# Attention ahead of two gated MLPs: normalization steps at the end of a turn, and weight decodes inside the turns

## The chip, the core and the metric

The kernel runs on one core of one Trainium2 chip. The metric is the device time of one execution in microseconds (us); lower is better. The engines are named as the profile names them: PE (TensorE matmul) and PEld (its weight loads), DVE (VectorE), ACT (ScalarE), POOL (GpSimd) and SP (SyncE, which issues nearly all DMAs here).

## The reference

Attention over 4 batches of 12 heads, 448 positions, head size 64; then two gated MLPs on 1792 tokens with 768 columns inside and 1536 hidden ones.

```python
def rmsnorm(x, g):
    rms = np.sqrt(np.mean(x * x, axis=-1, keepdims=True) + 1e-06)
    return x / rms * g
q_n, k_n = rmsnorm(q, g_q), rmsnorm(k, g_k)
scores = scale * np.matmul(q_n, k_n.transpose(0, 1, 3, 2))
scores = scores - np.max(scores, axis=-1, keepdims=True)
attn = np.exp(scores)
attn = attn / (np.sum(attn, axis=-1, keepdims=True) + 1e-09)
attn_out = np.matmul(attn, v)
...
x = (x @ w_a) * (x @ w_b) @ w_out                                # first MLP
x = (1 / (1 + np.exp(-(x @ w_gate)))) * (x @ w_val) @ w_out      # second MLP
```

The weights arrive as 64-bit floats, which the kernel reads as pairs of 32-bit words.

## The kernel before

**Attention in turns.** Two heads of one batch form a pair; there are 24 pairs. A table of steps, `turns`, is played once for each i from 1 to 22; `begin` stands before it and `end` behind it. A step is a small function with an offset: `(exp, 0, 4)` works on pair i, `(x_tr, -1, 0, 0)` on pair i-1. No scheduler moves anything: the order of the table is the order of the instructions on every engine, and each engine works strictly in order.

The steps of a pair, in the order of its life:

- `load`, `load_r`, `load_v` (SP): q, k and v.
- `squares` (POOL, L192 to L196): products and a first halving of the sum. L192 is one multiplication of 768 columns.
- `mean` (DVE, L203 reduces, L204 scales and adds), `rsqrt` (ACT, L211 Ln, L212 Exp), `newton` (DVE, L219 to L221): together the factor `y` of the normalization.
- `scale` (POOL, L230 and L243): q and k times `y`, into `qkn` and `qrem`. `t_tr` (PE, L254 to L259) transposes them into a PSUM buffer of the ring `tr`, which has 3 buffers.
- `k_hi` and `q_hi` (ACT, L278 and L264) and `k_lo` and `q_lo` (DVE, L288 and L269) split them into a high and a low part KH, KL, QH, QL. `k_ends` (POOL, L294) copies two small corners of KH and of KL.
- `s` (PE, L305): scores of one or two row tiles; `top` (DVE, L311): the negated row maximum `nm`; `exp` (ACT, L323): the exponentials P and their sums. The scores `s` have 4 PSUM banks for 7 tiles a turn, so a bank must be free of its `exp` before it is written again.
- A turn later, `x_tr` (PE, L333 to L341) transposes P into the ring `tr`; `x_out` copies it to SBUF, on ACT (L352) or on DVE (L350). `pv` (PE, L365) multiplies with v.
- `rsum` (DVE, L372 adds 1e-9 to 7 sums a row, L373 takes the reciprocal), `rsum_tr` (PE, L379), `rsum_post` (ACT, L384, then a DMA of the row to DRAM), `rsum_get` (SP, L393, three DMAs that broadcast it), `norm` (DVE, L400: `xs` = `pv` times `rs`) and `put` (SP, L405).
- `early_hi` and `early_lo` (ACT L422, POOL L428) prepare a first part of the MLP's input in six of the turns.

**Weights.** A quarter of a weight block (128x384) is loaded as `raw` (L611, 384 KB) and decoded: one ACT operation (L622), then L623, L625 and L629 on DVE. A decoded quarter, or a difference of two, is then split into `wh` (ACT, L717) and `wl` (DVE, L559). `prepare(l, e, n)` advances two generators, `decodes` and `splits`, by n small pieces; a whole decode takes four pieces. It decodes up to the eighth quarter and splits up to the fourth product before the MLP has begun. `decode` (L434) is the step that calls it; before, it stands ten times in `end`, and nowhere else. A `raw` is loaded when a decode ends, and waits on SP for the buffer that this decode read.

**MLP.** `first_part` walks over products (m, p), each 18 matmuls (L870) of a block of weights with one of seven combinations of the input's quadrants (a Strassen scheme). The first eight products need only inputs that attention has long stored; the ninth needs S1, the sum of two quadrants (`operands`, DVE L783, with the casts of L774 and the rests of L559). The quadrants come back from DRAM (`stage_in`, L755), some of them behind the last pair's `norm` and `put`.

Of the kernel before, what the change touches and what calls it, by code (L numbers as in the profile page):

```python
# [23 lines left out]
def attention_then_two_gated_mlps(  # L24
# [90 lines left out]
    def attention():  # L115
# [316 lines left out]
            begin_u()  # L432

        def decode(i, n):  # L434
            prepare(0, 3, 1)

        def close_s(i):
            sctx.close()
# [6 lines left out]
        def mlp(i, n):  # L445
# [11 lines left out]
            (exp, 0, 1), (top, 0, 5), (scale, 2, 1), (k_lo, 1), (k_ends, 1), (exp, 0, 5), (s, 0, 2), (s, 0, 3), (load, 4),  # L457
            (scale, 2, 0), (scale, 2, 2), (top, 0, 2), (load_r, 3), (exp, 0, 2), (top, 0, 6), (squares, 3),
            (exp, 0, 6), (top, 0, 3), (t_tr, 2, 1), (t_tr, 2, 0), (exp, 0, 3), (mean, 3), (k_hi, 2), (k_lo, 2),
            (q_hi, 2), (q_lo, 2), (k_ends, 2),  # L460
        )

        turns = (
            (rsum_get, -2), (early, 0), (put, -3), (s, 0, 0), (rsqrt, 2), (s, 0, 1), (newton, 2),
            (x_tr, -1, 0, 0), (x_tr, -1, 0, 1), (top, 0, 0), (exp, 0, 0), (rsum, -1), (x_out, -1, 0, 0), (top, 0, 4),
            (exp, 0, 4), (x_out, -1, 0, 1), (pv, -2, 1), (scale, 2, 1), (scale, 2, 0), (scale, 2, 2), (top, 0, 1),
            (exp, 0, 1), (load, 4), (load_r, 3), (load_v, 1), (x_tr, -1, 1, 0), (top, 0, 5), (x_out, -1, 1, 0),
            (x_tr, -1, 1, 1), (exp, 0, 5), (x_out, -1, 1, 1), (rsum_tr, -1), (norm, -2), (s, 0, 2), (rsum_post, -1),
            (s, 0, 3), (early_hi, -1), (squares, 3), (early_lo, -1), (x_tr, -1, 2, 0), (top, 0, 2), (x_out, -1, 2, 0),
            (exp, 0, 2), (x_tr, -1, 2, 1), (top, 0, 6), (exp, 0, 6), (x_out, -1, 2, 1), (pv, -1, 0), (top, 0, 3),  # L470
            (t_tr, 2, 1), (exp, 0, 3), (x_tr, -1, 3, 0), (k_hi, 2), (k_lo, 2), (t_tr, 2, 0), (x_out, -1, 3, 0),
            (q_hi, 2), (q_lo, 2), (mean, 3), (k_ends, 2),
        )

        end = (
# [4 lines left out]
            (x_tr, -2, 2, 0), (top, -1, 2), (x_out, -2, 2, 0), (exp, -1, 2), (x_tr, -2, 2, 1), (top, -1, 6),  # L480
            (exp, -1, 6), (x_out, -2, 2, 1), (put, -3), (close, -1), (pv, -2, 0), (top, -1, 3), (x_tr, -2, 3, 0),
            (exp, -1, 3), (x_out, -2, 3, 0), (rsum_get, -2), (decode, -1, 0), (decode, -1, 1), (x_tr, -1, 0, 0),
            (close_s, -1), (decode, -1, 2), (x_out, -1, 0, 0), (rsum, -1), (x_tr, -1, 0, 1), (decode, -1, 3),
            (pv, -2, 1), (x_out, -1, 0, 1), (decode, -1, 4), (x_tr, -1, 1, 0), (x_out, -1, 1, 0), (decode, -1, 5),
            (x_tr, -1, 1, 1), (norm, -2), (x_out, -1, 1, 1), (rsum_tr, -1), (decode, -1, 6), (put, -2), (decode, -1, 7),
            (rsum_post, -1), (x_tr, -1, 2, 0), (decode, -1, 8), (x_out, -1, 2, 0), (mlp, -1, 0),
# [242 lines left out]
    def prepare(l, e, n):  # L729

        if preps[l] is None:
            preps[l] = weights(l)
        decodes, splits = preps[l]
        must = n > NE
        while n > 0:
            n -= 1
            if must and done[l] >= e:
                break
            if decoded[l] < min(NE, max(EARLY * 2 - 1, done[l] + 3), e + 4):
                next(decodes, None)  # L740
            elif done[l] >= e:
                break
            if done[l] < e:
                next(splits, None)
# [505 lines left out]
```

## Time and profile before

| | before |
|---|---|
| median of 3 runs | 1281.25 us (1281.11 to 1281.63) |
| profiled execution, its own time | 1282.0 us |
| its span | 1280.2 us |
| PE, DVE, ACT, POOL busy | 95%, 73%, 51%, 14% of the span |
| mean granted clock of TensorE | 0.984 |

The span is the time from the first to the last instruction. A timeline row gives start, duration, engine, line, operation, tiles and how many instructions were merged into it; in square brackets stands how long the engine sat idle just before, and what ended that. Since a matmul's end is modelled, the distance of starts tells more about PE than its busy time.

### The profile page before, as it was taken

Reading aid. Unit: us, or ns where it says so; the run is one execution under the profiler, and the core shown is the slowest. Engines: PE = TensorE matmul, PEld = TensorE weight load, DVE = VectorE, ACT = ScalarE, POOL = GpSimd, SP = SyncE. Lnnn points to the kernel's source line nnn. Section 1 sums busy time; section 2 is a strip of 40 time slices with the busy share of each in tenths; the row PEclk is TensorE's granted clock in tenths of the full one; section 3 lists DMA queues with packets and bytes.
Section 4 is the critical chain, followed back from the end, with each engine's and each line's share of the span. In section 5 each row is a group of like instructions: output and inputs, shape, how many; then the busy total and the mean of one; then the engine's idle time right before and its main releaser. Section 6 shows DMA issues by size and latency. Waiting matters only on the chain.

```text
span 1280.2 us, 18150 instructions
## 1 busy us (share of the span) xinstructions
PE 1214.4 (95%) x6414; PEld 1018.7 (80%) x6414; DVE 939.2 (73%) x1617; ACT 656.8 (51%) x1267; POOL 181.7 (14%) x250
## 2 busy tenths in 40 slices
PE   4999999998879999999999998989999999999997
PEld 3556556565768888888888887878888888999997
DVE  6777777775787878777558698976877777558583
ACT  3667767775554443453345645553444453445543
POOL 4545556730000000000002022000000000000000
PEclk8899999999989999999999998999999999999999
DMA  5243344415614556556486464314556556477573
GB/s 126 59 113 92 93 124 119 121 61 181 242 52 138 174 158 192 162 174 197 163 284 223 152 199 136 115 52 138 175 165 191 163 168 195 168 279 253 180 253 112
DMA packets 142026, 203.00 MB, mean 159 GB/s; under 512 B 23240, under 2 KB 116592, under 8 KB 141936
## 3 DMA queue, kind: packets, MB, share of 16 engines
q1 hardware_dynamic: 140816, 201.27, 49.8%
q8 instruction: 50, 0.82, 0.3%
q10 hardware_dynamic: 1120, 0.59, 0.2%
q14 instruction: 40, 0.33, 0.1%
HBM read 147.46 MB, written 54.35 MB: 158 GB/s over the span
## 4 chain that ended last, share of the span: by engine, by line
PE 62%; DVE 6%; ACT 3%; issue 2%; DMA 1%; ACTq 0%; SPq 0%; DVEq 0%
PE mm L870 43%; PE mm L1122 10%; PE mm L1132 9%; DVE xl L559 2%; ACT gh L1039 1%; DVE wl L559 1%; DVE gl L559 0%; DVE d L1009 0%; DVE u L1027 0%; DVE u L783 0%; DVE d L705 0%; DVE al L783 0%; ACT wh L1012 0%; DVE u L894 0%; DVE d L629 0%
## 5 line engine op out<-in xcount | busy, mean ns | idle before, releaser
L870 PE MATMUL mm<-xh,wh 128*128 128x512 f32 (+1 forms) x1008 | 370.6, 368 | 15.4 <-ACT u L922 5.8
L870 PE MATMUL mm<-xl,wh 128*128 128x512 f32 (+1 forms) x1008 | 371.4, 368 | 5.4 <-DVE xl L559 5.4
L870 PE MATMUL mm<-xh,wl 128*128 128x512 f32 (+1 forms) x1008 | 372.2, 369 | 0.0
L559 DVE TENSOR_TENSOR wl<-d,wh 128x384 fp32r<-128x384 f32 x252 | 143.7, 571 | 154.8 <-ACT wh L717 94.1
L870 PEld LDWEIGHTS mm<-xh,wh 128*128 128x128 f32 x1008 | 191.2, 190 | 42.1 <-ACT u L922 6.7
L870 PEld LDWEIGHTS mm<-xl,wh 128*128 128x128 f32 x1008 | 190.8, 189 | 30.4 <-DVE xl L559 7.5
L870 PEld LDWEIGHTS mm<-xh,wl 128*128 128x128 f32 x1008 | 190.7, 189 | 21.1
L717 ACT CAST wh<-d 128x384 fp32r<-128x384 f32 x168 | 86.0, 512 | 174.0 <-DVE d L705 135.0
L323 ACT ACTIVATE P<-s,nm 128x448 f32<-128x448 f32 x168 | 106.0, 636 | 39.4 <-DVE nm L311 39.0
L1012 ACT CAST wh<-d 128x384 fp32r<-128x384 f32 x84 | 43.2, 514 | 150.0 <-DVE d L1009 52.6
L622 ACT ACTIVATE d<-raw 128x384 f32<-128x384 f32 x136 | 75.6, 557 | 71.8 <-DMA raw<-in_moe_w_a_dram 16.1
L311 DVE TENSOR_REDUCE nm<-s 128x1 f32<-128x448 f32 x168 | 98.1, 608 | 2.7 <-PE s L305 2.7
L1132 PE MATMUL mm<-wh,gh 128*128 128x384 f32 x294 | 98.8, 336 | 0.5 <-ACT ah L1155 0.3
L1132 PE MATMUL mm<-wl,gh 128*128 128x384 f32 x294 | 98.6, 335 | 0.0
L1132 PE MATMUL mm<-wh,gl 128*128 128x384 f32 x294 | 98.5, 335 | 0.0
L1122 PE MATMUL mm<-gh,wh 128*128 128x512 f32 x252 | 92.8, 368 | 5.1 <-ACT ah L1155 4.4
L1122 PE MATMUL mm<-gl,wh 128*128 128x512 f32 x252 | 93.5, 371 | 0.0
L1122 PE MATMUL mm<-gh,wl 128*128 128x512 f32 x252 | 93.1, 370 | 0.0
L559 DVE TENSOR_TENSOR gl<-u,gh 128x896 fp32r<-128x896 f32 x60 | 71.3, 1188 | 18.4 <-ACT gh L1039 18.3
L629 DVE SCALAR_TENSOR_TENSOR d<-d,raw 128x384 uint32<-128x384 uint32 x136 | 75.6, 556 | 10.9 <-ACT d L622 1.0
L625 DVE SCALAR_TENSOR_TENSOR raw<-raw 128x384 uint32<-128x384 uint32 x136 | 76.0, 559 | 4.1
L336 PE MATMUL tr<-ident,P 128*128 128x128 f32 x432 | 65.4, 279 | 13.7 <-ACT pt L352 13.2
(148 smaller groups left out, 1961.9 us busy)
## 6 DMA issues: line engine op xcount, KB each, us to landing
gd<-u SPq DMA_DIRECT2D x60, 448.0 KB
u<-gd SPq DMA_DIRECT2D x60, 448.0 KB
d<-wd SPq DMA_DIRECT2D x132, 192.0 KB
raw<-in_moe_w_out_dram SPq DMA_DIRECT2D x48, 384.0 KB
wd<-d SPq DMA_DIRECT2D x72, 192.0 KB
raw<-in_moe_w_val_dram SPq DMA_DIRECT2D x23, 384.0 KB
raw<-in_moe_w_a_dram SPq DMA_DIRECT2D x22, 384.0 KB
raw<-in_moe_w_b_dram SPq DMA_DIRECT2D x22, 384.0 KB
```

Of the source, the lines that this page charges most:

```text
L311: nc.vector.tensor_reduce(out=d["nm"][:, t:t + 1], in_=d["ps"][t], axis=AX.X, op=ALU.max, negate=True)
L323: nc.scalar.activation(out=e, in_=d["ps"].pop(t), func=AF.Exp, bias=d["nm"][:, t:t + 1], accum_out=d["sum"][:, t:t + 1])
L336: nc.tensor.transpose(tr[:, o + P * c:o + P * c + P], p[c][:, 512 * z + P * j:512 * z + P * j + P], ident)
L559: eng.tensor_tensor(out=lo, in0=t, in1=f32(hi), op=ALU.subtract)
L622: nc.scalar.activation(out=f32(t), in_=f32(high), func=AF.Copy, scale=2.0 ** -112)
L625: nc.vector.scalar_tensor_tensor(out=low, in0=high, scalar=0x80000000, in1=low, op0=ALU.bitwise_and, op1=ALU.bitwise_or)
L629: nc.vector.scalar_tensor_tensor(out=t, in0=t, scalar=3, in1=low, op0=ALU.logical_shift_left, op1=ALU.bitwise_or)
L717: nc.scalar.copy(out=hi, in_=t)
L870: nc.tensor.matmul(ps[:, o:o + size], w[:, P * c:P * c + P], x[:, o:o + size], start=(p in (1, 5) and c == 0 and z == 0), stop=(c == KC - ...
L1012: nc.scalar.copy(out=hi, in_=t)
L1122: nc.tensor.matmul(ps[:, o:o + size], w[:, P * un:P * un + P], g[:, o:o + size], start=(p in (1, 5) and f == 0 and z == 0), stop=(f == HF ...
L1132: nc.tensor.matmul(ps[:, o:o + HB], g[:, P * t:P * t + P], w, start=(p in (1, 5) and f == 0 and z == 0), stop=(f == HF - 1 and z == 2), sk ...
```

## The change

The steps `rsqrt` and `newton` of a pair follow directly on its `mean` at the end of a turn, in place of the start of the next turn. At a turn's start, the ACT copy `x_out` of the first transposed tile stands ahead of the first `exp`. `rsum` moves from behind the first `top` of the turn to behind the fourth, and `norm` ahead of the copy of tile (1, 1). `decode` stands twice in each turn, and does something from i = 6 on: 17 turns, 34 calls. The ten calls in `end` stay where they are.

```diff
         def decode(i, n):
-            prepare(0, 3, 1)
+            if i > 5:
+                prepare(0, 3, 1)
...
-            (q_hi, 2), (q_lo, 2), (k_ends, 2),
+            (rsqrt, 3), (q_hi, 2), (newton, 3), (q_lo, 2), (k_ends, 2),
         )
 
         turns = (
-            (rsum_get, -2), (early, 0), (put, -3), (s, 0, 0), (rsqrt, 2), (s, 0, 1), (newton, 2),
-            (x_tr, -1, 0, 0), (x_tr, -1, 0, 1), (top, 0, 0), (exp, 0, 0), (rsum, -1), (x_out, -1, 0, 0), (top, 0, 4),
+            (rsum_get, -2), (early, 0), (put, -3), (s, 0, 0), (s, 0, 1),
+            (x_tr, -1, 0, 0), (x_tr, -1, 0, 1), (top, 0, 0), (x_out, -1, 0, 0), (exp, 0, 0), (top, 0, 4),
...
-            (exp, 0, 1), (load, 4), (load_r, 3), (load_v, 1), (x_tr, -1, 1, 0), (top, 0, 5), (x_out, -1, 1, 0),
-            (x_tr, -1, 1, 1), (exp, 0, 5), (x_out, -1, 1, 1), (rsum_tr, -1), (norm, -2), (s, 0, 2), (rsum_post, -1),
-            (s, 0, 3), (early_hi, -1), (squares, 3), (early_lo, -1), (x_tr, -1, 2, 0), (top, 0, 2), (x_out, -1, 2, 0),
...
+            (exp, 0, 1), (load, 4), (load_r, 3), (load_v, 1), (x_tr, -1, 1, 0), (top, 0, 5), (rsum, -1), (exp, 0, 5),
+            (x_out, -1, 1, 0), (x_tr, -1, 1, 1), (norm, -2), (x_out, -1, 1, 1), (rsum_tr, -1), (s, 0, 2),
+            (rsum_post, -1), (s, 0, 3), (decode, 0, 0), (early_hi, -1), (squares, 3), (early_lo, -1), (x_tr, -1, 2, 0),
...
+            (pv, -1, 0), (top, 0, 3), (t_tr, 2, 1), (exp, 0, 3), (decode, 0, 1), (mean, 3), (rsqrt, 3), (x_tr, -1, 3, 0),
+            (k_hi, 2), (newton, 3), (k_lo, 2), (t_tr, 2, 0), (x_out, -1, 3, 0), (q_hi, 2), (q_lo, 2), (k_ends, 2),
```

The order of instructions shows three places. From line 436 on, the changed file's line numbers are higher by one.

DVE at the start of a turn, before: from the rest of q (QL) to the third row maximum, then now.

```order
L269 TENSOR_TENSOR QL<-tr,QH 128x512
L203 TENSOR_REDUCE ms<-sq 128x14
L204 TENSOR_SCALAR ms<-ms 128x14
L219 SCALAR_TENSOR_TENSOR t<-y 128x14
L220 TENSOR_TENSOR t<-t,ms 128x14
L221 SCALAR_TENSOR_TENSOR y<-t,y 128x14
L311 TENSOR_REDUCE nm<-s 128x1
L372 TENSOR_SCALAR rc<-sum 128x7
L373 RECIPROCAL rc<-rc 128x7
L311 TENSOR_REDUCE nm<-s 128x1
L350 COPY pt<-tr 128x384
L311 TENSOR_REDUCE nm<-s 128x1 x2
```

```order
L288 SCALAR_TENSOR_TENSOR KL<-tr,G,KH 128x448
L269 TENSOR_TENSOR QL<-tr,QH 128x512
L311 TENSOR_REDUCE nm<-s 128x1 x2
L350 COPY pt<-tr 128x384
L311 TENSOR_REDUCE nm<-s 128x1 x2
L372 TENSOR_SCALAR rc<-sum 128x7
L373 RECIPROCAL rc<-rc 128x7
L400 TENSOR_TENSOR xs<-pv,rs 128x448
L350 COPY pt<-tr 128x384
```

Five operations left the place between QL and the first maximum, and the two of `rsum` moved from behind the first maximum to behind the fourth.

DVE at the end of a turn, before and now (a turn with the second and third operation of a decode).

```order
L400 TENSOR_TENSOR xs<-pv,rs 128x448
L311 TENSOR_REDUCE nm<-s 128x1 x2
L350 COPY pt<-tr 128x384
L311 TENSOR_REDUCE nm<-s 128x1
L288 SCALAR_TENSOR_TENSOR KL<-tr,G,KH 128x448
L269 TENSOR_TENSOR QL<-tr,QH 128x512
```

```order
L626 SCALAR_TENSOR_TENSOR raw<-raw 128x384
L311 TENSOR_REDUCE nm<-s 128x1 x2
L350 COPY pt<-tr 128x384
L311 TENSOR_REDUCE nm<-s 128x1
L630 SCALAR_TENSOR_TENSOR d_3158<-d_3158,raw 128x384
L203 TENSOR_REDUCE ms<-sq 128x14
L204 TENSOR_SCALAR ms<-ms 128x14
L219 SCALAR_TENSOR_TENSOR t<-y 128x14
L220 TENSOR_TENSOR t<-t,ms 128x14
L221 SCALAR_TENSOR_TENSOR y<-t,y 128x14
L288 SCALAR_TENSOR_TENSOR KL<-tr,G,KH 128x448
```

Between the last maximum and KL stood nothing; now a piece of a decode and the five operations of `mean` and `newton` stand there, and another piece stands ahead of the third pair of maxima.

DVE where attention ends, from the last pair's last maximum on, before and now.

```order
L311 TENSOR_REDUCE nm<-s 128x1
L623 TENSOR_SCALAR raw<-raw 128x384
L625 SCALAR_TENSOR_TENSOR raw<-raw 128x384
L372 TENSOR_SCALAR rc<-sum 128x7
L373 RECIPROCAL rc<-rc 128x7
L629 SCALAR_TENSOR_TENSOR d_4204<-d_4204,raw 128x384
L350 COPY pt<-tr 128x384
L623 TENSOR_SCALAR raw<-raw 128x384
L559 TENSOR_TENSOR wl<-d_4204,wh 128x384
L400 TENSOR_TENSOR xs<-pv,rs 128x448
```

```order
L311 TENSOR_REDUCE nm<-s 128x1
L372 TENSOR_SCALAR rc<-sum 128x7
L373 RECIPROCAL rc<-rc 128x7
L350 COPY pt<-tr 128x384
L400 TENSOR_TENSOR xs<-pv,rs 128x448
L350 COPY pt<-tr 128x384 x2
L400 TENSOR_TENSOR xs<-pv,rs 128x448
L560 TENSOR_TENSOR wl<-d_2811,wh 128x384
L560 TENSOR_TENSOR wl<-d_3158,wh 128x384
L624 TENSOR_SCALAR raw<-raw 128x384
```

Up to the last pair's `norm` no decode stands on DVE any more; before, four whole decodes stood there. The first operation of a decode comes behind it.

## Rows read from the trace of the kernel before

**Rows 1.** Busy time by stretch: length, PE, PEld, DVE, ACT, POOL, clock, DMA share, GB/s.
```profile
300.00:330.00 30.00, 24.55 (x124) 17.33 (x123) 15.97 (x36) 12.98 (x26) 0.00 (x0) 1.00 0.86 280
330.00:360.00 30.00, 21.93 (x97) 17.77 (x96) 28.37 (x41) 14.50 (x22) 0.00 (x0) 0.92 0.53 177
```

**Rows 2.** Timeline of PE: `rsum_tr` of four turns, and a wait within one.
```profile
190.84 0.28 PE L379 MATMUL tr<-ident,rc 128*7 128x128 f32 x1
...
202.16 0.55 PE L336 MATMUL tr<-ident,P 128*128 128x128 f32 x3 [0.48 <-ACT pt L352]
...
202.61 0.28 PE L379 MATMUL tr<-ident,rc 128*7 128x128 f32 x1
...
273.90 0.28 PE L379 MATMUL tr<-ident,rc 128*7 128x128 f32 x1
...
284.90 0.27 PE L379 MATMUL tr<-ident,rc 128*7 128x128 f32 x1
```

**Rows 3.** Timeline of DVE and ACT around the start of a turn.
```profile
196.88 0.68 DVE L288 SCALAR_TENSOR_TENSOR KL<-tr,G,KH 128x448 fp32r<-128x448 f32 x1 [1.99 <-ACT KH L278]
...
197.79 0.69 DVE L269 TENSOR_TENSOR QL<-tr,QH 128x512 fp32r<-128x512 f32 x1 [0.23 <-ACT QH L264]
...
198.40 0.61 DVE L203 TENSOR_REDUCE ms<-sq 128x14 f32<-128x448 f32 x1
...
200.26 0.62 DVE L311 TENSOR_REDUCE nm<-s 128x1 f32<-128x448 f32 x1
...
200.79 0.58 DVE L372 TENSOR_SCALAR rc<-sum 128x7 f32<-128x7 f32 x1
200.91 0.64 ACT L323 ACTIVATE P<-s,nm 128x448 f32<-128x448 f32 x1 [1.19 <-DVE nm L311]
...
202.01 0.55 DVE L350 COPY pt<-tr 128x384 f32<-128x384 f32 x1
...
202.47 1.14 DVE L311 TENSOR_REDUCE nm<-s 128x1 f32<-128x448 f32 x2
```

**Rows 4.** Timeline of POOL: in the beginning, and in the same turn.
```profile
24.62 0.24 POOL L294 CAST KL<-KL 64x64 fp32r<-64x64 f32 x1
24.94 0.83 POOL L230 TENSOR_TENSOR qkn<-qk,y 128x384 f32<-128x384 f32 x1
...
197.63 0.24 POOL L294 CAST KL<-KL 64x64 fp32r<-64x64 f32 x1 [0.41 <-DVE KL L288]
200.51 1.62 POOL L230 TENSOR_TENSOR qkn<-qk,y 128x384 f32<-128x384 f32 x2 [2.65 <-PE pv L365]
...
203.59 1.47 POOL L192 TENSOR_TENSOR sq<-qk 128x768 f32<-128x768 f32 x1
```

**Rows 5.** Timeline: DVE beside a POOL operation in the beginning; `rsum` with POOL idle.
```profile
10.63 1.73 DVE L243 TENSOR_SCALAR qrem<-rqk,y 64x64 f32<-64x64 f32 x2
...
10.84 1.47 POOL L192 TENSOR_TENSOR sq<-qk 128x768 f32<-128x768 f32 x1 [8.23 <-DMA qk<-in_q_dram]
...
291.29 0.16 DVE L372 TENSOR_SCALAR rc<-sum 128x7 f32<-128x7 f32 x1
```

**Rows 6.** Timeline of DVE where attention ends and the MLP begins.
```profile
303.04 0.37 DVE L623 TENSOR_SCALAR raw<-raw 128x384 uint32<-128x384 uint32 x1 [4.62 <-DMA raw<-in_moe_w_a_dram]
...
317.54 0.62 DVE L400 TENSOR_TENSOR xs<-pv,rs 128x448 f32<-128x448 f32 x1 [4.16 <-DMA rs<-dr]
...
330.37 1.09 DVE L783 TENSOR_TENSOR fl<-fh 128x896 f32<-128x896 f32 x1 [2.62 <-DMA fh<-xd]
```

**Rows 7.** The chain that ended last, in order of time: start, duration, engine, tile, line.
```profile
371.09 1.09 DVE xl L559
372.23 267.69 PE mm L870 x1307
```

**Rows 8.** Groups of instructions: count, busy us, mean ns, idle time before.
```profile
L629 DVE SCALAR_TENSOR_TENSOR d<-d,raw 128x384 uint32<-128x384 uint32 x136 | 75.6, 556 | 10.9 <-ACT d L622 1.0
L623 DVE TENSOR_SCALAR raw<-raw 128x384 uint32<-128x384 uint32 x136 | 48.5, 357 | 27.6 <-DMA raw<-in_moe_w_b_dram 7.0 <-DMA raw<-in_moe_w_a_dram 6.6 <-DMA raw<-in_moe_w_val_dram 6.5
```

More of the change, by code (lines that the diff above doesn't have):

```diff
@@ L459, in attention @@
             (exp, 0, 6), (top, 0, 3), (t_tr, 2, 1), (t_tr, 2, 0), (exp, 0, 3), (mean, 3), (k_hi, 2), (k_lo, 2),
-            (q_hi, 2), (q_lo, 2), (k_ends, 2),
+            (rsqrt, 3), (q_hi, 2), (newton, 3), (q_lo, 2), (k_ends, 2),
         )
         turns = (
-            (rsum_get, -2), (early, 0), (put, -3), (s, 0, 0), (rsqrt, 2), (s, 0, 1), (newton, 2),
-            (x_tr, -1, 0, 0), (x_tr, -1, 0, 1), (top, 0, 0), (exp, 0, 0), (rsum, -1), (x_out, -1, 0, 0), (top, 0, 4),
+            (rsum_get, -2), (early, 0), (put, -3), (s, 0, 0), (s, 0, 1),
+            (x_tr, -1, 0, 0), (x_tr, -1, 0, 1), (top, 0, 0), (x_out, -1, 0, 0), (exp, 0, 0), (top, 0, 4),
             (exp, 0, 4), (x_out, -1, 0, 1), (pv, -2, 1), (scale, 2, 1), (scale, 2, 0), (scale, 2, 2), (top, 0, 1),
-            (exp, 0, 1), (load, 4), (load_r, 3), (load_v, 1), (x_tr, -1, 1, 0), (top, 0, 5), (x_out, -1, 1, 0),
-            (x_tr, -1, 1, 1), (exp, 0, 5), (x_out, -1, 1, 1), (rsum_tr, -1), (norm, -2), (s, 0, 2), (rsum_post, -1),
-            (s, 0, 3), (early_hi, -1), (squares, 3), (early_lo, -1), (x_tr, -1, 2, 0), (top, 0, 2), (x_out, -1, 2, 0),
-            (exp, 0, 2), (x_tr, -1, 2, 1), (top, 0, 6), (exp, 0, 6), (x_out, -1, 2, 1), (pv, -1, 0), (top, 0, 3),
-            (t_tr, 2, 1), (exp, 0, 3), (x_tr, -1, 3, 0), (k_hi, 2), (k_lo, 2), (t_tr, 2, 0), (x_out, -1, 3, 0),
-            (q_hi, 2), (q_lo, 2), (mean, 3), (k_ends, 2),
+            (exp, 0, 1), (load, 4), (load_r, 3), (load_v, 1), (x_tr, -1, 1, 0), (top, 0, 5), (rsum, -1), (exp, 0, 5),
+            (x_out, -1, 1, 0), (x_tr, -1, 1, 1), (norm, -2), (x_out, -1, 1, 1), (rsum_tr, -1), (s, 0, 2),
+            (rsum_post, -1), (s, 0, 3), (decode, 0, 0), (early_hi, -1), (squares, 3), (early_lo, -1), (x_tr, -1, 2, 0),
+            (top, 0, 2), (x_out, -1, 2, 0), (exp, 0, 2), (x_tr, -1, 2, 1), (top, 0, 6), (exp, 0, 6), (x_out, -1, 2, 1),
+            (pv, -1, 0), (top, 0, 3), (t_tr, 2, 1), (exp, 0, 3), (decode, 0, 1), (mean, 3), (rsqrt, 3), (x_tr, -1, 3, 0),
+            (k_hi, 2), (newton, 3), (k_lo, 2), (t_tr, 2, 0), (x_out, -1, 3, 0), (q_hi, 2), (q_lo, 2), (k_ends, 2),
         )
```

## The prediction

> **What bounds the kernel now.** I read the stretches first, then PE's order in one turn, then who holds PE up, then the chain that ended last. From the ninth product of the first MLP on, the chain is one piece of PE work for 268 us [rows 7]: what comes behind is shifted as a whole, and only two places can give time. The first is the turn of attention. PE's `rsum_tr` comes every 11.77 us (202.61 - 190.84) [rows 2]. In the last turn but one interval it is 11.00 (284.90 - 273.90): the same matmuls, transposes of the next pair included, but no `mean` and `newton` are left to stand at the start of that turn. So a turn holds about 0.77 us that these steps cost, and one such loss is visible: the second half of a transposed tile waits 0.48 us for an ACT copy [rows 2]. The second place is the start of the MLP: from 300 to 360 us PE is busy 24.55 and 21.93 of 30, DVE first 15.97, then 28.37, and the granted clock falls to 0.92 [rows 1]. The reader is to see two different limits there. DVE first waits: 4.62 us for a raw weight, with the last pair's copies and `rsum` queued behind, then 4.16 for the broadcast sums, then 2.62 for a stored quadrant [rows 6]. From 330.37, when that quadrant is there, to 372.18, the end of the last rest that PE waits for [rows 6, 7], it works without a pause.
>
> **The change part by part.**
>
> *`mean`, `rsqrt`, `newton`.* The same nine instructions, none added. Before, they filled DVE from 198.40 to 200.26, 1.86 us between QL and the first maximum, and ACT's first `exp` idled 1.19 us for it [rows 3]. Now they stand between the last maximum and KL, where DVE idled 1.99 us [rows 3]. 1.86 fits into 1.99, so I cost it at nothing there and at a gain of 1.86 at the start. If that cover goes (a decode piece takes part of it), KL is late; it feeds a pair two turns on, but it also holds a buffer of the ring, and POOL's `scale` starts behind KL's copy. `y` is now there before `scale`, so POOL no longer waits 2.65 us [rows 4]. On ACT, KH stands behind Ln and Exp and so behind `mean`.
>
> *The copy ahead of the first `exp`.* No instruction more. It removes the 0.48 us of [rows 2]. The first `exp` is then behind a copy of about 0.6 us, but has 1.86 us in hand. Cost nothing.
>
> *`rsum`, `norm`.* `rsum` leaves the chain in front of the second maximum. It is now 4.10 us behind KL: 0.91 to QL, 0.61 to the first maximum, then four maxima at 0.53 and one copy at 0.46 [rows 3]. `rsum_tr` needs it, and PE needs `rsum_tr` before the next scores: this is the tight spot of the new order. `norm` a copy earlier waits for sums that were issued in the turn before; I cost it at nothing.
>
> Together I take a turn without decodes at the 11.00 of [rows 2]. What it could be worth at the best is that all of PE's waits go; the nearest row is the same 11.00, and the wait of 0.48 says that up to that much again may be in it: 10.5. At the worst another wait takes its place: 11.77.
>
> *Decodes in the turns.* 34 pieces are eight decodes and four splits, which leave the start of the MLP. One decode is 0.36 + 0.56 + 0.56 = 1.47 us on DVE (L625 reads as L629) [rows 8] and one ACT operation of nearly 0.6; it covers two turns, so a turn gets 0.74 us of DVE. DVE's waits for KL are used up by `mean`, so part of it lies on the path: I take 0.1 us a turn, between 0 (all beside PE) and 0.74 (all on it), near the lower end, because PE and not DVE sets the 11.00. Each decode ends with a load of 384 KB that on SP waits for L629 and stands ahead of the next turn's three broadcasts of sums; `norm` has some 4 us from the turn's start to take that. The first decode's ACT operation meets its load fresh: once, about 1 us, in the range.
>
> Sum for attention: 20 full turns; 4 at 11.77 - 11.00 = 0.77 and 16 at 0.67: 3.1 + 10.7 = **14 us**. Bounds: 20 x 1.27 = 25, and a loss (rivals).
>
> *The start of the MLP.* Three terms lie on the path. (a) The last pair's copies no longer stand behind a raw weight; `rsum_tr` of that pair loses the PE waits behind it. DVE's wait was 4.62 us, but PE had other work in it; I take half, 2.3. (b) Behind that row's copy, SP held (by the order of its DMAs) four more raw loads ahead of the sums and the stored quadrants; each waits for a decode of 1.47. I take three of them as on the path: 4.4. So the first sum for the ninth product comes some 6.7 us earlier than 330.37. (c) From there on DVE works through; fewer decodes stand in it. Of the eleven that the order has between attention and the end of that piece eight are gone, but most of these lay ahead of 330; two of them, 2.9 us, are inside. That makes 9.6, **10 us**. Below: 5 (the quadrants come no sooner than DMA allows; 280 GB/s was moving [rows 1]). Above: PE's own idle time there, 30 - 24.55 + 30 - 21.93 = 13.5, and some for the clock: 16.
>
> Against the profiled execution's own 1282.0 us (span 1280.2 and 1.8 around it): 1282.0 - 14 - 10 = 1258. The median of the runs is 0.75 below that execution, so **1257 us**.
>
> **The rivals.**
>
> *A. `rsum` loses a race with POOL.* POOL's `scale` now starts behind KL's copy: 197.63 - 196.88 = 0.75 after KL, and 0.32 behind it (24.94 - 24.62), and the squares (L192) 3.08 after that (203.59 - 200.51) [rows 4]: 4.15 behind KL. `rsum` gets there at 4.10. The traces show what the loser pays: in the beginning two DVE operations of this kind took 1.73 us together; the second could not end before the 1.47 us of L192 on POOL were over [rows 5]. And `rsum` itself took 0.58 while POOL was in L230, 0.16 with POOL idle [rows 3, 5]. So a `rsum` 0.05 us too late ends at 4.15 + 1.47 = 5.62 in place of 4.27. PE's `rsum_tr` came 5.73 behind KL before (202.61 - 196.88), less its wait of 0.48 some 5.2; with the reciprocal of 0.2 and its way it would now be about 5.95: 0.75 late, and the turn 11.75. With a decode in the way, where there is no wait left to cover it, about 12.1. Then 16 turns lose 0.33 each: 1282.0 + 5 - 10 - 0.75 = **1276**. For it: the numbers above. Against it: by them `rsum` is first. The Trainium skill, SBUF — State Buffer, section "SBUF: two separate sides", speaks against this change: DVE in a two-port mode and POOL share a port pair as an exclusive lock, held for the whole instruction, and the other blocks entirely; it counts DVE operations with two SBUF inputs in as well. The trace agrees for L243 beside L192 (1.73 us). By that rule rival A's price is the whole of L192, and the result 1276; if the two could share, it would be my 1257.
>
> *B. Slower.* Every decode and split operation on DVE has SBUF inputs, like L243, and stands where POOL is now busy with `squares`. If A holds and each of the 28 operations (24 of decodes, 4 of splits) waits 0.6 us behind a POOL operation on top, less than half of L192, the turns lose another 17 us: 1276 + 17 = 1293. It decides from 0.2 us an operation on, where the gain of 6 us is gone. For it: the 1.73 [rows 5]. Against it: pieces at a turn's end meet an idle POOL, since `squares` are over before `mean`. I put it at **1289**.
>
> *C. The start of the MLP gives nothing.* The quadrants' loads take as long as before, and the ninth product begins at the same distance from attention's end. Then 1282.0 - 14 - 0.75 = **1267**. For it: DMA was busy for 0.86 of that stretch [rows 1]. Against it: a third of that traffic were the raw weights that are now loaded long before.
>
> **How the numbers follow.** Forecast 0.5, A 0.25, C 0.18, B 0.07. The forecast's own range is 1247 to 1265. For 8 in 10 the range has to take in C and A: from 1246 (attention at 20, MLP at 15) to 1278. A measurement of this kernel tells 0.2%, 2.6 us, from no change, so "same" is 1278.7 to 1283.8. Forecast and C are faster; A is so in four fifths of its spread, else the same; B is slower. Faster 0.87, same 0.06, slower 0.07.
>
> **What the profile of the changed kernel would show.** `rsum_tr` every 11.0 us up to the sixth turn and about 11.1 from there; no wait of L336 for the ACT copy; L372 of about 0.16 us in the turns (A: over 1 us, and PE's `rsum_tr` waiting for DVE); the first `exp` less than 3 us behind QL. Behind attention no DVE wait for a raw weight ahead of the last `rsum`; the first sum of quadrants some 7 us nearer to attention's end, and the ninth product's chain starting some 24 us sooner than 372.23. The forecast is wrong if turns are not shorter by 0.5 us or if the distance from the last turn to that chain stays.

## The result, and the profile after

The changed kernel takes **1261.31 us** (median of 4 runs, 1260.70 to 1262.13) beside 1281.44 for the kernel before (4 runs on the same chip): a ratio of 0.9843, 95% interval 0.983 to 0.9855. The forecast was 1257, with a range of 1246 to 1278. The profiled execution has a span of 1259.9 us, 20.3 less than before. From L436 on, line numbers of the changed kernel are one higher (L624 was L623).

| start, us | before | after | gain up to here |
|---|---|---|---|
| 22nd `rsum_tr`, of the last full turn | 284.90 | 272.89 | 12.0 |
| 24th `rsum_tr`, of the last pair | 305.26 | 290.95 | 14.3 |
| first sum of quadrants, L783 (L784) | 330.37 | 312.19 | 18.2 |
| chain of the ninth product | 372.23 | 351.79 | 20.4 |
| end of the span | 1280.2 | 1259.9 | 20.3 |

So attention gave 12.0 and the start of the MLP 8.4; behind the chain's start nothing changed. But the turns are of four kinds, which this timeline of PE shows (`rsum_tr`; start, duration, operation, idle time before it and what ended that):

```profile
81.49 0.27 PE L379 MATMUL tr<-ident,rc 128*7 128x128 f32 x1
92.23 0.27 PE L379 MATMUL tr<-ident,rc 128*7 128x128 f32 x1
105.58 0.27 PE L379 MATMUL tr<-ident,rc 128*7 128x128 f32 x1 [0.65 <-DVE rc L373]
116.32 0.27 PE L379 MATMUL tr<-ident,rc 128*7 128x128 f32 x1
127.32 0.27 PE L379 MATMUL tr<-ident,rc 128*7 128x128 f32 x1
...
204.63 0.27 PE L379 MATMUL tr<-ident,rc 128*7 128x128 f32 x1 [0.65 <-DVE rc L373]
215.92 0.27 PE L379 MATMUL tr<-ident,rc 128*7 128x128 f32 x1 [0.41 <-DVE rc L373]
```

Turns without a decode take 10.74 us. The turn of the first decode takes 13.35. The next eight take 10.74 to 11.02, and the six turns of `early_hi` and `early_lo` 11.8 or 11.3. The 13.35 is read from one row of DVE and one of ACT: both sat idle for the first raw weight, and PE's next transposes waited for an ACT copy behind it. (The run with the load sooner, below, tests this.)

```profile
98.72 0.36 DVE L624 TENSOR_SCALAR raw<-raw 128x384 uint32<-128x384 uint32 x1 [2.71 <-DMA raw<-in_moe_w_a_dram]
98.72 0.56 ACT L623 ACTIVATE d<-raw 128x384 f32<-128x384 f32 x1 [1.69 <-DMA raw<-in_moe_w_a_dram]
101.38 0.33 PE L333 MATMUL tr<-ident,P 128*128 128x128 f32 x1 [1.74 <-ACT pt L352]
```

In the turns of `early_lo` it is POOL. The timeline of DVE and POOL there:

```profile
195.63 2.09 POOL L428 TENSOR_TENSOR xl<-xst,xh 128x896 fp32r<-128x896 f32 x1
196.51 1.63 DVE L630 SCALAR_TENSOR_TENSOR d<-d,raw 128x384 uint32<-128x384 uint32 x1
198.06 0.61 DVE L203 TENSOR_REDUCE ms<-sq 128x14 f32<-128x448 f32 x1
...
207.13 2.08 POOL L428 TENSOR_TENSOR xl<-xst,xh 128x896 fp32r<-128x896 f32 x1
208.33 1.10 DVE L624 TENSOR_SCALAR raw<-raw 128x384 uint32<-128x384 uint32 x1
209.35 0.61 DVE L203 TENSOR_REDUCE ms<-sq 128x14 f32<-128x448 f32 x1
```

L630 takes 1.63 us in place of 0.56 and L624 1.10 in place of 0.36: neither ends before L428 does. `mean` (L203) stands behind them, then KL, the maxima and `rsum`, for which PE waited 0.65 and 0.41 above.

The race of rival A, in a turn with decodes, DVE and POOL:

```profile
133.42 0.68 DVE L288 SCALAR_TENSOR_TENSOR KL<-tr,G,KH 128x448 fp32r<-128x448 f32 x1
...
137.52 0.16 DVE L372 TENSOR_SCALAR rc<-sum 128x7 f32<-128x7 f32 x1
137.55 1.47 POOL L192 TENSOR_TENSOR sq<-qk 128x768 f32<-128x768 f32 x1
```

`rsum` (L372) starts 4.10 us behind KL and L192 4.13: the prediction had 4.10 and 4.15. `rsum` is first by 0.03 us here (by 0.00 to 0.03 in the turns) and takes 0.16 in every turn.

The stretches of [rows 1] after the change, and the end of the chain of [rows 7]:

```profile
300.00:330.00 30.00, 27.94 (x136) 24.32 (x135) 20.31 (x31) 13.71 (x21) 0.00 (x0) 1.00 0.63 222
330.00:360.00 30.00, 23.13 (x89) 18.55 (x88) 26.18 (x36) 17.36 (x25) 0.00 (x0) 0.83 0.17 55
```

```profile
350.65 1.10 DVE xl L560
...
351.79 267.68 PE mm L871 x1307
```

PE has 3.4 us more work in 300 to 330, DMA 0.63 in place of 0.86, and ahead of the first sum DVE waits for no raw weight and no quadrant (before: 4.62 and 2.62 us, [rows 6]). DVE and ACT:

```profile
299.75 0.62 DVE L400 TENSOR_TENSOR xs<-pv,rs 128x448 f32<-128x448 f32 x1 [3.41 <-PE pv L365]
307.26 0.35 DVE L624 TENSOR_SCALAR raw<-raw 128x384 uint32<-128x384 uint32 x1
...
310.37 0.91 ACT L923 COPY u<-mm 128x896 f32<-128x896 f32 x1 [3.15 <-PE mm L871]
...
311.71 0.56 DVE L560 TENSOR_TENSOR wl<-d,wh 128x384 fp32r<-128x384 f32 x1 [2.84 <-ACT wh L718]
312.19 1.08 DVE L784 TENSOR_TENSOR fl<-fh 128x896 f32<-128x896 f32 x1
```

What the sum stands behind now is the kernel's own order: on DVE the split of a weight, which waits 2.84 us for ACT's `wh`, and on ACT a copy that waits 3.15 us for a product of PE. The granted clock of the second stretch is 0.83 (before 0.92), and the chain behind it is as long as before (267.68 and 267.69).

### The profile page after: what moved, and what is told of

Read it like the earlier page. It is cut to its first block, busy times and chain, and to the rows that moved or that the text cites. A ratio compares the mean times of both kernels' runs of the same rounds, so it can differ in the third digit from the quotient of the medians.

```text
span 1259.9 us, 18180 instructions
## 1 busy us (share of the span) xinstructions
PE 1206.6 (96%) x6414; PEld 1016.9 (81%) x6414; DVE 941.0 (75%) x1617; ACT 653.0 (52%) x1267; POOL 183.8 (15%) x250
## 4 chain that ended last, share of the span: by engine, by line
PE 80%; DVE 10%; ACT 4%; issue 2%; DMA 2%; POOL 1%; SPq 0%; ACTq 0%; DVEq 0%; POOLq 0%
PE mm L871 45%; PE mm L1123 10%; PE mm L1133 9%; PE pv L365 5%; PE s L305 5%; PE tr L336 3%; DVE xl L560 2%; DVE nm L311 2%; PE tr L254 1%; PE tr L333 1%; ACT gh L1040 1%; DVE d L630 1%; DMA d<-wd 1%; DVE wl L560 1%; DVE QL L269 1%
## 5 line engine op out<-in xcount | busy, mean ns | idle before, releaser
L623 ACT ACTIVATE d<-raw 128x384 f32<-128x384 f32 x140 | 78.1, 558 | 65.0 <-DMA raw<-in_moe_w_a_dram 15.0
L323 ACT ACTIVATE P<-s,nm 128x448 f32<-128x448 f32 x168 | 104.9, 635 | 12.1 <-DVE nm L311 12.1
L630 DVE SCALAR_TENSOR_TENSOR d<-d,raw 128x384 uint32<-128x384 uint32 x140 | 81.2, 580 | 10.9 <-ACT d L623 1.3
L352 ACT COPY pt<-tr 128x512 f32<-128x512 f32 x96 | 54.8, 571 | 51.6 <-PE tr L336 47.7
L626 DVE SCALAR_TENSOR_TENSOR raw<-raw 128x384 uint32<-128x384 uint32 x140 | 78.2, 558 | 4.1
```

Of the source, the lines that this page charges most:

```text
L323: nc.scalar.activation(out=e, in_=d["ps"].pop(t), func=AF.Exp, bias=d["nm"][:, t:t + 1], accum_out=d["sum"][:, t:t + 1])
L623: nc.scalar.activation(out=f32(t), in_=f32(high), func=AF.Copy, scale=2.0 ** -112)
L626: nc.vector.scalar_tensor_tensor(out=low, in0=high, scalar=0x80000000, in1=low, op0=ALU.bitwise_and, op1=ALU.bitwise_or)
L630: nc.vector.scalar_tensor_tensor(out=t, in0=t, scalar=3, in1=low, op0=ALU.logical_shift_left, op1=ALU.bitwise_or)
```

## The experiments

Eleven kernels were run. Ratios are to the kernel before, run on the same chip. The last two columns split the profiled execution: from the second to the 22nd `rsum_tr` (20 turns), and from there to the span's end.

| kernel | median, us | ratio, 95% interval | 20 turns | from there to the end |
|---|---|---|---|---|
| before | 1281.44 | | 235.35 | 995.3 |
| changed | 1261.31 | 0.9843, 0.983 to 0.9855 | 223.60 | 987.0 |
| order alone | 1260.77 | 0.985, 0.9831 to 0.987 | 214.73 | 995.7 |
| decodes alone | 1278.58 | 0.998, 0.9971 to 0.9989 | 241.96 | 987.2 |
| `rsum` late | 1281.83 | 1.0, 0.9989 to 1.001 | 242.59 | 987.7 |
| first `exp` ahead of the copy | 1260.85 | 0.9843, 0.9828 to 0.9858 | 222.49 | 987.2 |
| no late piece beside `early_lo` | 1256.49 | 0.9799, 0.9782 to 0.9816 | 218.17 | 988.6 |
| load sooner | 1258.70 | 0.9822, 0.9807 to 0.9836 | 221.15 | 986.4 |
| piece in the root's wait | 1254.06 | 0.9785, 0.9769 to 0.9801 | 216.66 | 986.9 |
| the last two together | 1253.17 | 0.9782, 0.9768 to 0.9796 | 215.36 | 987.2 |
| `mean` alone | 1260.72 | 0.9831, 0.9814 to 0.9847 | 214.73 | 997.4 |
| `rsum` alone | 1291.62 | 1.0075, 1.006 to 1.009 | 243.83 | 995.0 |
| `mean` and decodes placed | 1253.57 | 0.9779, 0.9766 to 0.9792 | 214.95 | 988.2 |

### The two halves of the change

```diff
         def decode(i, n):
-            if i > 5:
+            if i > 22:
                 prepare(0, 3, 1)
```

> The new order with none of the 34 decode pieces in the turns (the end keeps its ten decode steps, as before). Theory: the two parts of the change are separate and add up. Then rsum_tr comes every 10.73 us from the third turn to the last, also in the turns of early_hi and early_lo; its 22nd is 21 us sooner than before (some 264 in place of 284.90), and from there to the first quadrant sum and to the ninth product's chain it takes what it took before (45.5 and 87.3 us). Time 1261, the same as with the decodes: what the decodes bring the MLP (8.4 us) they cost the turns. Rival: a decode costs a turn no more than the 0.13 us that the turns of 10.74 and 11.00 show, and what lengthens the early turns is the early operations themselves. Then the turns of early_hi stay at 11.5, the 22nd rsum_tr is at 268, and the time is 1266.

Measured: 1260.77, every turn 10.72 to 10.75, 22nd `rsum_tr` at 263.28, first sum 45.8 us behind it (before 45.5). The theory holds. Busy time by stretch, inside the turns (length, then PE, PEld, DVE, ACT, POOL, clock, DMA share, GB/s):

```profile
120.00:180.00 60.00, 60.00 (x410) 38.29 (x406) 49.95 (x112) 43.36 (x127) 37.41 (x58) 1.00 0.41 113
180.00:262.00 82.00, 82.00 (x561) 52.44 (x560) 66.89 (x149) 65.46 (x181) 54.23 (x75) 1.00 0.41 115
```

The first of these stretches in the kernel before:

```profile
120.00:180.00 60.00, 56.96 (x375) 35.69 (x373) 45.61 (x104) 42.36 (x118) 32.70 (x53) 1.00 0.33 95
```

PE is now busy for the whole of both stretches, and no wait of PE is left in them: 10.73 is PE's own work of a turn. The decodes in the turns add 223.60 - 214.73 = 8.9 us there and take 995.7 - 987.0 = 8.7 from what follows: as the change places them, they bring nothing.

The other half, in the order of before:

```diff
         def decode(i, n):
-            prepare(0, 3, 1)
+            if i > 5:
+                prepare(0, 3, 1)
...
-            (s, 0, 3), (early_hi, -1), (squares, 3), (early_lo, -1), (x_tr, -1, 2, 0), (top, 0, 2), (x_out, -1, 2, 0),
+            (s, 0, 3), (decode, 0, 0), (early_hi, -1), (squares, 3), (early_lo, -1), (x_tr, -1, 2, 0), (top, 0, 2), (x_out, -1, 2, 0),
...
-            (t_tr, 2, 1), (exp, 0, 3), (x_tr, -1, 3, 0), (k_hi, 2), (k_lo, 2), (t_tr, 2, 0), (x_out, -1, 3, 0),
+            (t_tr, 2, 1), (exp, 0, 3), (decode, 0, 1), (x_tr, -1, 3, 0), (k_hi, 2), (k_lo, 2), (t_tr, 2, 0), (x_out, -1, 3, 0),
```

> The order of before with the 34 decode pieces at the changed kernel's places (behind the fourth score product and behind the last exp, from the sixth turn on). Theory: the start of the MLP gains its 8.4 us whatever the order of the turns, and the second piece of a turn lies in DVE's wait for KL (1.99 us) and costs nothing; the first decode still waits 2.7 us for its load. First quadrant sum 38 to 40 us behind the 22nd rsum_tr in place of 45.5; attention 2 to 5 us longer; time 1276 to 1279. Rival: without the new order the pieces come on top of DVE's chain of a turn, by 0.74 us in each of 16 turns; attention 12 us longer, time 1285.

Measured: 1278.58. The first sum stands 39.3 us behind the 22nd `rsum_tr`, as in the changed kernel; the 20 turns are 6.6 longer. The theory holds for the MLP, and its 2 to 5 us for the turns were too few: 3.6 of the 6.6 lie in the two turns of the first decode (13.73 and 13.37 in place of 11.77). So the gain at the MLP's start needs the decodes and not the order. DVE's wait for KL hid part of the pieces: of its 1.99 us, 1.38 or 0.85 are left in the plain turns.

### What the order owes to which move

```diff
-            (rsum_get, -2), (early, 0), (put, -3), (s, 0, 0), (rsqrt, 2), (s, 0, 1), (newton, 2),
+            (rsum_get, -2), (early, 0), (put, -3), (s, 0, 0), (s, 0, 1),
...
-            (t_tr, 2, 1), (exp, 0, 3), (x_tr, -1, 3, 0), (k_hi, 2), (k_lo, 2), (t_tr, 2, 0), (x_out, -1, 3, 0),
-            (q_hi, 2), (q_lo, 2), (mean, 3), (k_ends, 2),
+            (t_tr, 2, 1), (exp, 0, 3), (mean, 3), (rsqrt, 3), (x_tr, -1, 3, 0), (k_hi, 2), (newton, 3), (k_lo, 2), (t_tr, 2, 0), (x_out, -1, 3, 0),
+            (q_hi, 2), (q_lo, 2), (k_ends, 2),
```

(`begin` ends as in the changed kernel.)

> The kernel before with mean, rsqrt and newton alone moved to the turn's end; rsum and norm where they were, no decodes in the turns. Theory: the move takes 1.86 us off the time from KL to the first maximum and is the larger part of the 1.04 us that a turn gained in the order alone; rsum, still in front of the second maximum, keeps its 0.58 beside L230 on POOL. Turns of 10.8 to 11.2, time 1262 to 1269. Rival: rsum in front of the second maximum still sets the turn (PE's rsum_tr does not come sooner than POOL and the copies let it); turns of 11.4 to 11.77, time 1274 to 1281.

Measured: 1260.72, turns of 10.72 to 10.75, below the 10.8 of the theory: `mean` is not the larger part, it is all of it. `rsum` stands in front of the second maximum as before, beside L230 on POOL, and is slow, and it costs nothing, as DVE and POOL here show:

```profile
140.09 1.63 POOL L230 TENSOR_TENSOR qkn<-qk,y 128x384 f32<-128x384 f32 x2
...
141.07 0.67 DVE L372 TENSOR_SCALAR rc<-sum 128x7 f32<-128x7 f32 x1
...
144.19 0.56 DVE L350 COPY pt<-tr 128x384 f32<-128x384 f32 x1 [0.19 <-PE tr L336]
```

The pair of L230 ends at 141.72, `rsum` at 141.74; a few operations on, DVE waits for PE.

```diff
-            (x_tr, -1, 0, 0), (x_tr, -1, 0, 1), (top, 0, 0), (exp, 0, 0), (rsum, -1), (x_out, -1, 0, 0), (top, 0, 4),
+            (x_tr, -1, 0, 0), (x_tr, -1, 0, 1), (top, 0, 0), (exp, 0, 0), (x_out, -1, 0, 0), (top, 0, 4),
...
-            (exp, 0, 1), (load, 4), (load_r, 3), (load_v, 1), (x_tr, -1, 1, 0), (top, 0, 5), (x_out, -1, 1, 0),
-            (x_tr, -1, 1, 1), (exp, 0, 5), (x_out, -1, 1, 1), (rsum_tr, -1), (norm, -2), (s, 0, 2), (rsum_post, -1),
+            (exp, 0, 1), (load, 4), (load_r, 3), (load_v, 1), (x_tr, -1, 1, 0), (top, 0, 5), (rsum, -1), (exp, 0, 5),
+            (x_out, -1, 1, 0), (x_tr, -1, 1, 1), (norm, -2), (x_out, -1, 1, 1), (rsum_tr, -1), (s, 0, 2), (rsum_post, -1),
```

> The kernel before with rsum and norm alone moved to their new places (rsum behind the fourth maximum and the copy, norm a copy sooner); mean, rsqrt and newton stay at the turn's start. Theory: rsum then stands some 6.0 us behind KL (4.10 and the 1.86 of the nine operations), rsum_tr at 6.4 in place of 5.73; it is the mean move that makes room for this one, and alone it loses: turns of 12.0 to 12.5, time 1286 to 1296. Rival: rsum leaves the way in front of the second maximum, where it took 0.58 and 0.2; the maxima come sooner, and turns shorten to 11.2 to 11.6, time 1269 to 1278.

Measured: 1291.62, turns of 12.27. `rsum` starts 5.97 us behind KL, as forecast; PE's `rsum_tr`, 6.51 behind KL, waits in each turn:

```profile
129.59 0.68 DVE L288 SCALAR_TENSOR_TENSOR KL<-tr,G,KH 128x448 fp32r<-128x448 f32 x1 [1.99 <-ACT KH L278]
...
135.56 0.16 DVE L372 TENSOR_SCALAR rc<-sum 128x7 f32<-128x7 f32 x1
...
136.09 0.27 PE L379 MATMUL tr<-ident,rc 128*7 128x128 f32 x1 [0.92 <-ACT P L323]
```

The theory holds: the move of `rsum` lives on the room that `mean` made. (The row names ACT's P, whose sum was read out at 136.06, behind the end of the reciprocal at 135.95. But PE's weight load for `rsum_tr` starts 0.12 us behind the reciprocal, as it does in the changed kernel where the row names DVE, so it is the reciprocal that PE waited for.)

```diff
-            (x_tr, -1, 0, 0), (x_tr, -1, 0, 1), (top, 0, 0), (x_out, -1, 0, 0), (exp, 0, 0), (top, 0, 4),
+            (x_tr, -1, 0, 0), (x_tr, -1, 0, 1), (top, 0, 0), (exp, 0, 0), (x_out, -1, 0, 0), (top, 0, 4),
```

> The changed kernel with the first exp ahead of the first copy of a turn again, as before. Theory: the wait of PE for that copy comes back with 0.3 to 0.6 us a turn (it was 0.48), and the turn grows by about that: 11.0 to 11.2 in place of 10.73; time 1267 to 1273. Rival: with the first maximum 1.86 us sooner, the exp is through before the copy's transposes are there, and the swap is worth nothing: turns of 10.73 to 10.8, time 1261 to 1262.

Measured: 1260.85, turns ahead of the first decode 10.72 to 10.75. The rival holds: once the first maximum comes sooner, the copy is no longer late behind the `exp`, and the swap is worth nothing. (The 1.1 us in the table are the turn of the first decode, 12.19 here.)

### The race on the port

```diff
-            (exp, 0, 1), (load, 4), (load_r, 3), (load_v, 1), (x_tr, -1, 1, 0), (top, 0, 5), (rsum, -1), (exp, 0, 5),
-            (x_out, -1, 1, 0), (x_tr, -1, 1, 1), (norm, -2), (x_out, -1, 1, 1), (rsum_tr, -1), (s, 0, 2),
+            (exp, 0, 1), (load, 4), (load_r, 3), (load_v, 1), (x_tr, -1, 1, 0), (top, 0, 5), (exp, 0, 5),
+            (x_out, -1, 1, 0), (x_tr, -1, 1, 1), (norm, -2), (rsum, -1), (x_out, -1, 1, 1), (rsum_tr, -1), (s, 0, 2),
```

> The changed kernel with rsum behind norm in place of ahead of it, so that it starts some 4.7 us behind KL and thus inside L192 on POOL (4.13 to 5.60 behind KL). Theory (rival A of the prediction was a true danger, missed by 0.03 us): L372 takes about 1.0 us in place of 0.16, as it ends with L192; rsum_tr stands 1.3 us later behind KL (6.0 in place of 4.65), PE waits for rc in every turn, and a turn is 11.5 to 12.0; time 1275 to 1287. Rival (the two engines share): L372 stays at 0.16 to 0.3, rsum_tr is 0.55 us later, which PE partly has; turns 10.75 to 11.3; time 1262 to 1272.

Measured: 1281.83; the whole gain is lost. Turns are 11.77 ahead of the decodes, 12.85 and 13.59 at the first decode, then 12.1 to 12.4, and 11.34 and 11.11 at the end; the prediction's rival A had 11.75 and 12.1. DVE, POOL and PE in one turn:

```profile
183.49 0.62 DVE L400 TENSOR_TENSOR xs<-pv,rs 128x448 f32<-128x448 f32 x1
183.51 1.47 POOL L192 TENSOR_TENSOR sq<-qk 128x768 f32<-128x768 f32 x1
184.02 0.99 DVE L372 TENSOR_SCALAR rc<-sum 128x7 f32<-128x7 f32 x1
...
185.39 0.27 PE L379 MATMUL tr<-ident,rc 128*7 128x128 f32 x1 [1.50 <-DVE rc L373]
```

L192 ends at 184.98 and `rsum` at 185.01. The theory holds. This is the rule of the Trainium skill, SBUF — State Buffer, section "SBUF: two separate sides": of a GpSimd operation and a DVE operation in a two-port mode, or one with two SBUF inputs against a GpSimd operation that reads SBUF, the one that starts first has the shared port pair for its whole instruction. The trace agrees (0.99 us in place of 0.16); whether L372 ran in such a mode, no run shows. `norm` (L400, one input in PSUM and one in SBUF) starts at the same time as L192 and takes its usual 0.62.

### The three losses of the decodes

```diff
         def decode(i, n):
-            if i > 5:
+            if i > 5 and not (n == 1 and 14 < i < 21):
                 prepare(0, 3, 1)
```

> The changed kernel without the second decode piece in the six turns of early_hi and early_lo (six of 34 pieces go back to the end). Theory: these turns are 11.8 and 11.3 because that piece (L624 1.10, L630 1.63 us) waits for L428 on POOL. Without it they are 10.75 to 10.9; 22nd rsum_tr 4 to 5 us sooner (268 to 269 in place of 272.9); the start of the MLP gives back 1.5 to 2.5 of its 8.4. Time 1258 to 1259.5. Rival: it is the number of pieces and not the lock; with one piece in place of two the turns still take 11.2, attention gains 2 us and the MLP loses 2: time 1261.

Measured: 1256.49, the six turns at 10.72 to 10.75 with one piece in each, and the later part only 1.6 us longer. The theory holds, and was too modest: with these pieces gone the whole 4.9 us of the six turns are gone. This run takes away the piece together with its wait; that it was its place behind L428, and not one piece more, the run with the piece in the root's wait shows, where the six turns hold both pieces and take 10.72 to 10.83.

```diff
         def decode(i, n):
-            if i > 5:
+            if i > 6 or (i, n) in ((5, 1), (6, 1)):
                 prepare(0, 3, 1)
```

> The changed kernel with the two first loads of raw weights issued half a turn to a turn sooner (at the second place of the turn ahead), the pieces unmoved. Theory: the turn of 13.34 is one wait of 2.7 us for that load; now 10.7 to 11.0, all else as before, time 1258.7. Rival: the turn's length comes from what stands behind the load on SP; then the turn ahead of it grows in its place and the time stays at 1261.

Measured: 1258.70; the turn of 13.35 takes 10.82, and DVE's wait of 2.71 us for the load is gone:

```profile
95.47 0.37 DVE L624 TENSOR_SCALAR raw<-raw 128x384 uint32<-128x384 uint32 x1
```

The theory holds. (The loads stand one whole turn sooner on SP: 1.3 us behind the `rsum_tr` of the turn ahead.)

```diff
-            (pv, -1, 0), (top, 0, 3), (t_tr, 2, 1), (exp, 0, 3), (decode, 0, 1), (mean, 3), (rsqrt, 3), (x_tr, -1, 3, 0),
+            (pv, -1, 0), (top, 0, 3), (t_tr, 2, 1), (exp, 0, 3), (mean, 3), (rsqrt, 3), (decode, 0, 1), (x_tr, -1, 3, 0),
```

> The changed kernel with the second piece of a turn between rsqrt and newton in place of ahead of mean. Theory: DVE waits there 0.6 to 0.7 us a turn for ACT's root, room for L624 (0.36) or L630 (0.55), and L428 on POOL is nearly over by then. So turns of 10.73 to 10.8 from the seventh on, also with early_hi; 22nd rsum_tr 6 to 7 us sooner (266 to 267); the MLP's start stays as in the changed kernel. Time 1254.5 to 1255.5. Rival: the piece's ACT operation (0.58 us) now stands between the root and KH and makes KL late; turns of 11.0 to 11.3, time 1260 to 1262.

Measured: 1254.06, turns of 10.71 to 10.83 from the eighth on. The 22nd `rsum_tr` is at 264.77, 2 us sooner than the theory had. DVE and POOL in a turn of `early_lo`:

```profile
202.61 2.09 POOL L428 TENSOR_TENSOR xl<-xst,xh 128x896 fp32r<-128x896 f32 x1
...
203.85 0.61 DVE L203 TENSOR_REDUCE ms<-sq 128x14 f32<-128x448 f32 x1
204.50 0.23 DVE L204 TENSOR_SCALAR ms<-ms 128x14 f32<-128x14 f32 x1
204.65 0.35 DVE L624 TENSOR_SCALAR raw<-raw 128x384 uint32<-128x384 uint32 x1
205.35 0.17 DVE L219 SCALAR_TENSOR_TENSOR t<-y 128x14 f32<-128x14 f32 x1 [0.35 <-ACT y L212]
```

The reduction of `mean` runs beside L428 at its usual 0.61; the piece starts as L428 ends and fills a wait for ACT's root, of which 0.35 is left.

> Both of the two runs before together. If the two theories hold, no turn is longer than 10.9 from the third on; the 22nd rsum_tr comes at 264 to 265, as in the order alone (263.3), and the MLP keeps its 8.4: time 1252 to 1253. If the rivals of both hold: 1260 to 1262. If one: 1255 to 1259.

Measured: 1253.17, turns of 10.72 to 10.84, 22nd `rsum_tr` at 263.23. Both theories hold in the trace. The median is 0.9 us below the run before it, with intervals that overlap: putting the piece later had already taken the first decode's turn to 12.24, so less was left for the load. It beats the changed kernel: 0.9768 to 0.9796 against 0.983 to 0.9855.

> The kernel before with three edits only: mean, rsqrt and newton at the turn's end, the decode pieces in the turns with the second one between rsqrt and newton, and the first loads sooner. rsum, norm and the first exp stay where they were before. Theory: the moves of rsum, norm and the copy are worth nothing in the turns, also with decodes in them; turns of 10.7 to 10.85, 22nd rsum_tr at 262 to 264, time 1252 to 1254 as with all moves. Rival: with 1 us of pieces more on DVE a turn, the 0.67 of rsum in front of the second maximum counts: from the seventh turn on 11.1 to 11.4, time 1258 to 1263.

Its edits are those of `mean` alone, with the pieces and the first loads placed as in the run before it. Measured: 1253.57, turns of 10.71 to 10.78 from the third to all but the last, which takes 10.94. The theory holds: three edits give as much as all moves together (1253.17, the intervals overlap), without the near tie of `rsum` and L192.

## Why the prediction was right, and where its sum was not

**The sign, the size and the two places** were right: 20.1 us by the medians where 24 were forecast. The sum was 14 + 10; it is 12.0 + 8.4. But the 12.0 is 21 less 9, where the prediction had 15.4 less 1.6: the gain was mis-sized by 5 us and the cost by 7, and that these two errors largely cancel in the total is luck.

**The moves (term 11.00 for a turn without decodes): too small a gain.** A turn is 10.73, between the 10.5 and the 11.00 that the prediction gave. The 11.00 was the one turn at attention's end [rows 2]; what the turn comes down to when PE never waits had no row of its own before, and in the order alone PE has no wait left. So the order is worth 235.35 - 214.73 = 20.6 in 20 turns, where 15.4 was in the sum (20 x 0.77).

**Which move does it.** The prediction gave `mean` 1.86 us in front of the first maximum and the copy the 0.48. The runs show the first to be the whole, and the copy and `rsum` to be worth nothing: with `mean` out of the way, PE waits at neither of these places any more. In the changed kernel ACT's first `exp` of a turn starts 1.5 us behind QL (135.82 and 134.33), where it started 3.1 behind it [rows 3], and the copy's lateness went with that.

**"I take 0.1 us a turn" for the decodes: the step that failed.** It was 8.9 us in all, some 0.55 a turn. It falls apart into 2.6 for the first load (forecast "once, about 1 us"), 1.3 in the eight turns after it (0.16 each, close to the 0.1), and 4.9 in the six turns of `early_lo` (0.82 each), where 0.6 was in. For these six the prediction had the mechanism, but in rival B and against another POOL operation: "pieces at a turn's end meet an idle POOL, since `squares` are over before `mean`". That is so where `squares` is POOL's last work; in the six turns L428 stands behind it. The trace of before has L428 in these turns; its place beside the new piece was not looked for.

**Rival A.** Not reached, though the starts stand 0.03 us apart: 4.10 and 4.13 behind KL. `rsum` a step later shows its price to have been right: 11.77 and 12.1 to 12.4 for 11.75 and 12.1. That 0.05 us of delay would already have cost it, no run shows for `rsum` and L192; the nearest rows are below, under the hardware. (Rival B's working gives 1293; the 1289 beside it has none.)

**The start of the MLP.** From the 22nd to the 24th `rsum_tr` 2.3 us less (term a: 2.3, a half that was a choice, so the match is partly luck); from there to the first sum 3.9 less (term b: 4.4); from there to the chain 2.3 less (term c: 2.9). For b the cause was right and its place half wrong: a raw load on SP held the last row's DMA itself, which ACT had ready at 306.37, until 308.56 (after: 291.61 and 291.64), so 2.6 of the 3.9 lie ahead of that DMA and 1.3 behind it, where the term had all. For c, DVE has 9 operations of decodes there in place of 14. Rival C is out. The decodes alone show that these terms belong to the decodes and not to the order.

**The signs announced.** No wait of PE's L336 for ACT's copy, L372 at 0.16 and no wait for a raw weight ahead of the last `rsum`: so. Turns of "11.1 from there": not so in seven of them. The chain 24 us sooner: 20.4.

## What to carry to other kernels

A change that gives a known total can still hide a part that loses what another gains: run each half alone before either is kept, since here the decodes as placed and the moves of `rsum`, `norm` and the copy were worth nothing, and one of these had put `rsum` where half a microsecond more costs 20. Work that is to fill a wait belongs into the wait itself (here DVE's 0.6 us for ACT's root), not ahead of it, and its place must be read against what the neighbour engine does in every kind of turn, not in the plainest one. The first use of a stream of loads needs its load issued a step before, or all engines behind it pay for it once.

## What the runs showed of the hardware

A near tie of DVE and POOL can go either way. In the order alone `rsum` and L192 start within 0.02 us of each other in every turn from the second on, since both follow KL at a fixed distance. Once L192 starts first, by 0.007 us (DVE and POOL, one row each):

```profile
112.12 1.49 POOL L192 TENSOR_TENSOR sq<-qk 128x768 f32<-128x768 f32 x1
112.13 0.16 DVE L372 TENSOR_SCALAR rc<-sum 128x7 f32<-128x7 f32 x1
```

`rsum` keeps its 0.16, and L192 takes 1.49 in place of 1.47. In the decodes alone, the first operation of a decode starts behind L428 twice, once by 0.014 us and once by 0.013:

```profile
222.09 2.33 POOL L428 TENSOR_TENSOR xl<-xst,xh 128x896 fp32r<-128x896 f32 x1
222.11 0.36 DVE L624 TENSOR_SCALAR raw<-raw 128x384 uint32<-128x384 uint32 x1
...
246.53 2.10 POOL L428 TENSOR_TENSOR xl<-xst,xh 128x896 fp32r<-128x896 f32 x1
246.55 2.30 DVE L624 TENSOR_SCALAR raw<-raw 128x384 uint32<-128x384 uint32 x1
```

The first time POOL loses 0.23 us, the second time DVE loses 1.94. In the run without late pieces, a start 0.06 us behind POOL's L193 was too late as well (L626 at 235.27, 0.75 in place of 0.55). So by the starts that the profile gives, a DVE operation gets in up to about 0.01 us behind the start of a POOL operation, and `rsum`, first by 0.00 to 0.03 us in the changed kernel, has no more than some 0.04 us to spare in any turn. A DVE operation can also get in between two POOL operations that stand back to back, and then POOL waits; in the changed kernel, with L192 ending at 128.27:

```profile
128.15 0.55 DVE L626 SCALAR_TENSOR_TENSOR raw<-raw 128x384 uint32<-128x384 uint32 x1
128.23 0.73 POOL L193 TENSOR_TENSOR sq<-rqk 128x128 f32<-128x128 f32 x1
```

L193 takes 0.40 where DVE leaves it alone. In these rows POOL's loss is the time from its start to the end of the DVE operation, less some 0.14 us (an estimate from the three: 0.03, 0.23 and 0.33 lost, with DVE ending 0.17, 0.38 and 0.47 behind POOL's start), which is why the 0.16 of `rsum` costs L192 next to nothing. And what is blocked by a POOL operation is not all of DVE: beside L428 and L192 the copies from PSUM, `norm` and the reduction of `mean` ran at their usual times, while L204 (0.60 for 0.17, in the run with the piece in the root's wait), L372, L624 and L630 did not.
